# Attention on one core: the last key tile's product with V as two 64-column halves

## The chip, the cores and the metric

The kernel runs on one core of one Trainium2 chip. The metric is the device time in microseconds (us) of one launch; lower is better. Three runs of the kernel before gave a median of 579.14 us (578.97 to 582.09).

## The reference

Four batches, eight heads, 576 positions, head dimension 64, everything in float32. Attention with a position bias is followed by a mixture of experts that takes one expert per token:

```python
scores = scale * np.matmul(q, k.transpose(0, 1, 3, 2))
...
h = np.maximum(x @ w1 + b1, 0.0)
bias = h @ w2
scores = scores + bias.transpose(2, 0, 1)[None, :, :, :]
scores = scores - np.max(scores, axis=-1, keepdims=True)
attn = np.exp(scores)
attn = attn / (np.sum(attn, axis=-1, keepdims=True) + 1e-09)
return np.matmul(attn, v).astype(np.float32)
```

The second half picks an expert `e` for each token from a gate and computes `p[e] * (np.maximum(x @ w1[e], 0) @ w2[e])`. The change concerns only `np.matmul(attn, v)`.

## The kernel before

Heads are taken two at a time: a pair `(p, b)` is two heads `x = 0, 1` of batch `b`. The 576 queries of a pair are five tiles `qt` (four of 128 rows, one of 64 in which both heads share the 128 partitions). For a query tile and head, `emit_s` makes the scores with fp16 matmuls (lines 305 and 306; line 316 for the tile of 64), VectorE adds the bias and takes the row extreme (line 325, one instruction and a short read of its accumulator), and ScalarE takes the exponential (line 330). `emit_t` turns the exponentials over in four transposes on TensorE (line 389) that ScalarE copies out (lines 395 and 393) into `eT`, plus one for key tile 4, the last 64 keys of both heads (lines 403 and 405), which VectorE copies into slot 8 of `eT` (line 406).

`emit_av(p, b, g)` then multiplies with V for a group `g` of query tiles: 256 queries for `g = 0`, 320 for `g = 1`. V is the stationary operand and `eT` the moving one, both float32; a float32 matmul shows as two records in the trace. The result `av` has head 0 in partitions 0 to 63 and head 1 in 64 to 127. Key tiles 0 to 3 belong to one head each, so each is one matmul onto 64 of the 128 columns of TensorE (line 420, `128*64` in the profile), head 0 and head 1 in turn, eight in all. Key tile 4 holds keys of head 0 in its upper 64 rows and keys of head 1 in its lower 64; its V, `vt[:, 4]`, has zeros where head and rows don't match, so one matmul over all 128 columns (line 417, `128*128`) serves both heads and stands first. For `g = 1` a small matmul with 64 columns (line 416) that folds two row sums stands in front of it. VectorE copies `av` out into `xt` (line 429, and line 431 for the folded sums); `av` is a single buffer. `emit_rows` turns `xt` over again (lines 443 and 445).

There are 16 pairs. Eight of them (the list `DMP`) do group 0 in another way, in fp16 with a transposing DMA (lines 346, 350, and 360 to 373 in `emit_lo` and `av_pieces`), so `emit_av` is called 24 times: 8 for `g = 0`, 16 for `g = 1`.

What sets the order: up to the last three units of the attention part the program's text does not. A scheduler takes the instructions of all steps and gives each engine its own order from costs of its own; SyncE's is fixed in the stretch of the `DMP` pairs, and everything from the last three units on stands as it is written. So the matmuls of one `emit_av` call can be parted by matmuls of other steps, and a change of one of them can move instructions on other engines.

## Time and profile before

| | |
|---|---|
| median of three runs | 579.14 us (578.97 to 582.09) |
| the profiled execution: its own time, its span | 580.73 us, 578.9 us |
| PE (TensorE matmul) busy | 533.2 us, 92% of the span |
| DVE (VectorE) busy | 464.8 us, 80% |
| ACT (ScalarE) busy | 436.5 us, 75% |
| POOL (GpSimd) busy | 269.7 us, 47% |
| mean granted TensorE clock | 0.983 of full speed |

The profiled execution's own time is the span and 1.8 us around it. The bias and first scores take the time up to about 60 us, attention goes on to about 340 us, and the experts take the rest. A busy PE is not PE at its peak: matmuls are pipelined, and the end of each is modelled. So the time that a matmul really takes from the engine is read from the starts of neighbours.

### The profile page before, as it was taken

What the parts mean: (1) busy time and instruction counts of PE and PEld (TensorE: products, weight loads), DVE (VectorE), ACT (ScalarE), POOL (GpSimd) and SP (SyncE); (2) the same over time, 40 slices, a digit from 0 to 9 for tenths busy, and PEclk for the clock granted to TensorE, in tenths of its full rate; (3) what the DMA queues carried; (4) which work ended last, traced back from release to release, by engine and by line L of the source; (5) the groups of instructions that cost most, each with busy time, mean ns of one, the idle gap of its engine ahead of it and who ended that gap; (6) DMA issues with size and microseconds to landing.
All of it is one profiled execution on the core that took longest, in us unless ns stands there. A gap on an engine that the chain in (4) does not pass through costs nothing. (4 is left out here: it accounts for less than half of the span.)

```text
span 578.9 us, 14247 instructions
## 1 busy us (share of the span) xinstructions
PE 533.2 (92%) x5302; PEld 358.7 (62%) x5319; DVE 464.8 (80%) x913; ACT 436.5 (75%) x743; POOL 269.7 (47%) x293
## 2 busy tenths in 40 slices
PE   4667999999999999999999999999999999999992
PEld 1223445665666667767577777487776867777851
DVE  7986886688888888787977558869999799897960
ACT  5876887866978877877689965468998787886940
POOL 5200000695199969966744760622344554344111
PEclk9998999999999999999999998799999999999997
DMA  8765447765698799845165002765999968889050
GB/s 284 257 183 166 116 138 209 235 201 145 168 246 226 194 259 241 224 103 151 62 243 154 11 23 59 241 227 194 296 269 267 336 155 214 156 214 236 16 185 30
DMA packets 99613, 106.15 MB, mean 183 GB/s; under 512 B 66893, under 2 KB 76239, under 8 KB 95442
## 3 DMA queue, kind: packets, MB, share of 16 engines
q1 hardware_dynamic: 94752, 89.45, 55.4%
q0 software_dynamic: 4640, 15.43, 8.9%
q8 instruction: 44, 0.72, 0.5%
q14 instruction: 31, 0.25, 0.2%
q10 hardware_dynamic: 146, 0.30, 0.2%
HBM read 128.92 MB, written 20.80 MB: 259 GB/s over the span
## 5 line engine op out<-in xcount | busy, mean ns | idle before, releaser
L330 ACT ACTIVATE e<-e,st 128x576 f32<-128x576 f32 x144 | 111.6, 776 | 14.4 <-DVE st L325 13.2
L325 DVE CUSTOM_DVE_ANT_0 e<-sps,wb 128x576 f32<-128x576 f32 x144 | 106.8, 750 | 16.9 <-PE sps L306 8.1
L1002 POOL DMA_INDIRECT out_dram<-y,odx x17 | 34.2, 2011 | 85.6 <-ACT y L992 45.5
L305 PE MATMUL sps<-kh,qs 128*128 128x288 f16 x256 | 68.5, 289 | 5.5 <-DVE st L325 3.9
L905 DVE TENSOR_TENSOR w<-wb,w 128x2048 bf16<-128x2048 f32 (+1 forms) x36 | 72.2, 2048 | 1.6 <-ACT w L898 1.4
L389 PE MATMUL ta<-c_cpb,e 128*128 128x128 f32 x448 | 71.2, 280 | 0.9 <-ACT e L330 0.4
L395 ACT COPY eT<-ta 128x512 f32<-128x512 f32 x96 | 54.9, 581 | 21.4 <-PE ta L389 20.0
L306 PE MATMUL sps<-kl,qs 128*128 128x288 f16 x256 | 67.8, 287 | 0.0
L976 PE MATMUL yp<-w,hhT 128*128 128x512 f16 (+1 forms) x255 | 64.4, 384 | 1.1 <-issue 0.2
L898 ACT CAST w<-wb 128x2048 f16<-128x2048 f32 (+1 forms) x40 | 63.8, 1639 | 2.2 <-DMA wb<-in_w_dram 1.3
L420 PE MATMUL av<-eT,vt 128*64 128x320 f32 (+1 forms) x384 | 62.4, 424 | 0.0
L937 PEld LDWEIGHTS <-we 128*128 128x128 f16 (+1 forms) x1056 | 59.9, 98 | 3.0 <-issue 0.5
L937 PE MATMUL sps<-xT,we 128*128 128x128 f16 (+1 forms) x1056 | 61.2, 219 | 0.0
L389 PEld LDWEIGHTS ta<-c_cpb,e 128*128 128x128 f32 x448 | 52.3, 142 | 12.8 <-ACT eT L395 3.0
L210 PE MATMUL sps<-hd,c_cpa 128*32 128x512 f32 (+17 forms) x352 | 43.7, 494 | 17.4 <-DVE hd L196 10.7
L196 DVE TENSOR_SCALAR hd<-tab,bp 128x448 f32<-128x448 f32 (+17 forms) x129 | 49.9, 446 | 5.0 <-PE sps L210 4.7
L937 PE MATMUL sps<-xT,wb 128*128 128x128 f16 (+3 forms) x1056 | 50.1, 209 | 0.6 <-issue 0.6
L937 PEld LDWEIGHTS <-wb 128*128 128x128 f16 (+1 forms) x1056 | 48.1, 99 | 3.7 <-issue 2.4
L905 DVE TENSOR_TENSOR we<-ws,we 128x2048 bf16<-128x2048 f32 (+1 forms) x25 | 48.7, 1985 | 0.0
L976 PEld LDWEIGHTS <-hhT 128*128 128x128 f16 x272 | 26.2, 100 | 29.9 <-issue 2.6
L118 POOL TENSOR_TENSOR qs<-qf,qs 64x288 f16<-64x288 f32 x48 | 42.8, 911 | 1.7
L420 PEld LDWEIGHTS av<-eT,vt 128*64 128x64 f32 x384 | 26.9, 136 | 26.5 <-issue 8.7
(234 smaller groups left out, 1013.9 us busy)
## 6 DMA issues: line engine op xcount, KB each, us to landing
ws<-in_w_dram SPq DMA_DIRECT2D x34, 1024.0 KB
wb<-in_w_dram SPq DMA_DIRECT2D x34, 1024.0 KB
hs<-in_w_dram SPq DMA_DIRECT2D x20, 1024.0 KB
bias_d<-bv SPq DMA_DIRECT2D x36, 295.5 KB
kf<-in_kt_dram SPq DMA_DIRECT2D x24, 288.0 KB
wb<-bias_d SPq DMA_DIRECT2D x16, 288.0 KB
wb<-bias_d SPq DMA_DIRECT2D x16, 256.0 KB
xrow_d<-xo SPq DMA_DIRECT2D x16, 256.0 KB
```

What stands on the lines that cost most here:

```text
L196: nc.vector.tensor_scalar(out=hd[:, 0:n], in0=tab[:, 0:n], scalar1=bp[:, k:k + 1], scalar2=0.0, op0=ALU.add, op1=ALU.max,)
L305: nc.tensor.matmul(out=ps[:, half, 0:288], lhsT=lq, rhs=kh[:, j], start=True, stop=False)
L306: nc.tensor.matmul(out=ps[:, half, 0:288], lhsT=lq, rhs=kl[:, j], start=False, stop=True)
L325: nc.vector.tensor_tensor_reduce(out=e, in0=ps[:, :, 0:288], in1=bsl, scale=-0.125, scalar=1e30, op0=ALU.add, op1=ALU.min, accum_out=st[:, ...
L330: nc.scalar.activation(out=e, in_=e, func=AF.Exp, scale=-1.0, bias=st[:, 0:1], accum_out=sm)
L389: nc.tensor.transpose(out=ta[:, j, :], in_=e[:, o:o + 128], identity=ident)
L395: nc.scalar.copy(out=eTv[:, :, hh, o:o + 128], in_=ta)
L420: nc.tensor.matmul(out=av[64 * x:64 * x + 64, 0:n], lhsT=vt[:, j, 64 * x:64 * x + 64], rhs=eT[:, 2 * j + x, 0:n], start=False, stop=(j == 3),)
L898: nc.scalar.copy(out=wh[c][:, sl], in_=src)
L905: nc.vector.tensor_tensor(out=wl[c][:, sl], in0=src, in1=wh[c][:, sl], op=ALU.subtract)
L937: nc.tensor.matmul(out=hp.rearrange("p a j -> p (a j)")[:, n * f:n * f + n], lhsT=w[f // 4][:, o:o + 128], rhs=x[:, kt], start=(i == 0), s ...
L976: nc.tensor.matmul(out=yp, lhsT=x[:, kt], rhs=w[kt // 4][:, 512 * (kt % 4):512 * (kt % 4) + 512], start=(i == 0), stop=(i == len(terms) - 1),)
```

## The change

The full-width matmul of key tile 4 goes. In its place two matmuls of 64 columns each, one per head, stand in front of the others, in one loop with them. They read the same rows of `eT` and the two column halves of the same `vt[:, 4]`.

```diff
         if g == 1:
             av_t[p, b] = av
             nc.tensor.matmul(out=av[0:64, 320:322], lhsT=fold, rhs=hs_t.pop((p, b)), start=True, stop=True)
-        nc.tensor.matmul(out=av[:, 0:n], lhsT=vt[:, 4], rhs=eT[:, 8, 0:n], start=True, stop=False)
-        for j in range(4):
+        for j in (4, 0, 1, 2, 3):
             for x in range(2):
                 nc.tensor.matmul(
                     out=av[64 * x:64 * x + 64, 0:n], lhsT=vt[:, j, 64 * x:64 * x + 64],
-                    rhs=eT[:, 2 * j + x, 0:n], start=False, stop=(j == 3),
+                    rhs=eT[:, 8 if j == 4 else 2 * j + x, 0:n], start=(j == 4), stop=(j == 3),
                 )
```

In the changed file the matmuls of the loop are line 419, and every later line has a number one lower (442 for 443, and so on). In the lists below an engine's instructions stand in its order, with line, operation, output and inputs, and the size of the output; "x8" is eight in a row.

TensorE, one `emit_av` call with `g = 1` at about 138 us. Before:

```order
L443 MATMUL ta<-c_cpb,xt 128x128 x4
L445 MATMUL tb_r<-c_cpb,xt 64x128
L416 MATMUL av<-hs,c_cpb 64x2
L417 MATMUL av<-eT,vt 128x320
L420 MATMUL av<-eT,vt 64x320 x8
L488 MATMUL sps<-xt,c_cpb 32x288 x6
```

And with the change:

```order
L442 MATMUL ta<-c_cpb,xt 128x128 x4
L444 MATMUL tb_r<-c_cpb,xt 64x128
L416 MATMUL av<-hs,c_cpb 64x2
L419 MATMUL av<-eT,vt 64x320 x10
L487 MATMUL sps<-xt,c_cpb 32x288 x6
```

Here all ten halves follow the small matmul of line 416, and no full-width matmul stands between.

TensorE, the first `emit_av` call with `g = 1`, at about 111 us. Before:

```order
L306 MATMUL sps<-kl,qs 128x288
L417 MATMUL av<-eT,vt 128x320
L389 MATMUL ta<-c_cpb,e 128x128 x4
L420 MATMUL av<-eT,vt 64x320 x8
L305 LDWEIGHTS qs
```

And with the change:

```order
L306 MATMUL sps<-kl,qs 128x288
L419 MATMUL av<-eT,vt 64x320
L389 MATMUL ta<-c_cpb,e 128x128 x4
L419 MATMUL av<-eT,vt 64x320 x9
L305 LDWEIGHTS qs
```

The first half took the place of the full-width matmul, four transposes stand behind it, and the second half of key tile 4 is the first of the nine that follow.

VectorE at about 153 us, in the stretch of the `DMP` pairs (`e_1933` and `e_1941` are the same fp16 buffer under two numbers). Before:

```order
L373 COPY xt<-av 128x256
L325 ISA e,st<-sps,wb_127 128x576
L325 ISA st 128x1
L346 TENSOR_TENSOR e_1933<-e,e_1933 128x1152
L406 COPY eT<-tb_r 128x64
```

And with the change:

```order
L373 COPY xt<-av 128x256
L325 ISA e,st<-sps,wb_127 128x576
L325 ISA st 128x1
L406 COPY eT<-tb_r 128x64
L325 ISA e,st<-sps,wb_127 128x576
L325 ISA st 128x1
L346 TENSOR_TENSOR e_1941<-e,e_1941 128x1152
```

The copy into slot 8 of `eT` now stands in front of the subtraction of line 346, and so does the next tile's instruction of line 325.

## Rows read from the trace of the kernel before

**Rows 1.** Busy time by stretch; columns PE, PEld, DVE, ACT, POOL, clock, DMA, GB/s.

```profile
60.00:105.00 45.00, 44.44 (x372) 23.60 (x368) 33.91 (x92) 36.07 (x84) 0.50 (x4) 1.00 0.59 168
105.00:150.00 45.00, 42.16 (x332) 27.62 (x330) 36.37 (x93) 32.16 (x75) 31.63 (x40) 1.00 0.65 187
150.00:265.00 115.00, 110.70 (x947) 76.20 (x944) 96.66 (x255) 95.15 (x220) 89.97 (x98) 1.00 0.80 202
265.00:340.00 75.00, 73.67 (x598) 51.16 (x596) 52.26 (x167) 59.78 (x132) 48.46 (x68) 1.00 0.37 118
```

**Rows 2.** Lines 420 and 417: records, shortest, median and longest ns, first and last start.

```profile
L420 PE MATMUL av<-eT,vt x384: 379/432/484, 63.7 to 338.7; 128*64 128x320 f32 x128, 128*64 128x256 f32 x64
...
L417 PE MATMUL av<-eT,vt x48: 379/432/537, 63.2 to 336.3; 128*128 128x320 f32 x32, 128*128 128x256 f32 x16
```

**Rows 3.** Order of time on PE, 111 to 115 us: start, duration, instruction, records.

```profile
111.31 0.70 PE L417 MATMUL av<-eT,vt 128*128 128x320 f32 x2
111.85 0.60 PE L389 MATMUL ta<-c_cpb,e 128*128 128x128 f32 x4
112.38 2.37 PE L420 MATMUL av<-eT,vt 128*64 128x320 f32 x16
114.69 0.30 PE L305 MATMUL sps<-kh,qs 128*128 128x288 f16 x1
```

**Rows 4.** Order of time on PE, 93 to 96 us, with 256 queries.

```profile
93.35 0.65 PE L420 MATMUL av<-eT,vt 128*64 128x256 f32 x4
93.93 1.28 PE L210 MATMUL sps<-hd,c_cpa 128*32 128x512 f32 x16
95.14 0.65 PE L420 MATMUL av<-eT,vt 128*64 128x256 f32 x2
95.72 0.44 PE L389 MATMUL ta<-c_cpb,e 128*128 128x128 f32 x2
```

**Rows 5.** Order of time on PE, 153 to 157 us.

```profile
153.94 0.28 PE L305 MATMUL sps<-kh,qs 128*128 128x288 f16 x1
154.06 0.28 PE L306 MATMUL sps<-kl,qs 128*128 128x288 f16 x1
155.17 0.81 PE L417 MATMUL av<-eT,vt 128*128 128x320 f32 x2 [0.82 <-DVE eT L406]
155.91 0.75 PE L420 MATMUL av<-eT,vt 128*64 128x320 f32 x2
156.59 0.30 PE L305 MATMUL sps<-kh,qs 128*128 128x288 f16 x1
```

**Rows 6.** Order of time on PE, 138 to 142 us.

```profile
138.31 0.28 PE L416 MATMUL av<-hs,c_cpb 128*64 128x2 f32 x2
138.52 0.81 PE L417 MATMUL av<-eT,vt 128*128 128x320 f32 x2
139.25 2.37 PE L420 MATMUL av<-eT,vt 128*64 128x320 f32 x16
141.56 1.82 PE L488 MATMUL sps<-xt,c_cpb 128*32 128x288 f32 x12
```

**Rows 7.** Order of time on PE, 266 to 267 us.

```profile
266.25 0.81 PE L417 MATMUL av<-eT,vt 128*128 128x320 f32 x2
266.90 0.60 PE L389 MATMUL ta<-c_cpb,e 128*128 128x128 f32 x4
```

**Rows 8.** Order of time on DVE, 153 to 156 us.

```profile
153.56 0.08 DVE L325 DVE_READ_ACCUMULATOR2_ANT st<- 128x1 f32 x1
153.62 1.36 DVE L346 TENSOR_TENSOR e<-e,e 128x1152 f16<-128x1152 f32 x1
154.90 0.22 DVE L406 COPY eT<-tb_r 128x64 f32<-128x64 f32 x1
155.03 0.75 DVE L325 CUSTOM_DVE_ANT_0 e<-sps,wb 128x576 f32<-128x576 f32 x1
```

**Rows 9.** Order of time on PE, 166 to 168 us: the next use of the transposing DMA's result.

```profile
166.87 0.49 PE L360 MATMUL av<-eT,v 128*128 128x256 f16 x3
```

**Rows 10.** Waits on PE, 105 to 340 us: us in total, times, longest.

```profile
PE av L417 <- DVE eT L406: 1.7, 3, 0.8
...
PE av L416 <- DVE xt L373: 0.7, 1, 0.7
```

**Rows 11.** Busy time by stretch, behind the attention part; columns as in rows 1.

```profile
354.00:361.00 7.00, 7.00 (x69) 4.93 (x66) 6.90 (x13) 3.16 (x9) 0.00 (x0) 0.76 0.24 37
```

## The prediction

> **What bounds the kernel now.** I began with busy time by stretch, because the change sits in attention alone. [...] The idle time left in 150 to 265 us is 115 - 110.70 = 4.3 us; no order of work can win more there. Line 417 has 48 records, two to a matmul, hence 24 calls, and line 420 has 384, hence 192 halves [rows 2]. What each costs I then read from starts in order of time, not from durations, which overlap.

> **Prices, from starts.** A full-width matmul of 320 queries between other full-width work holds PE for 111.85 - 111.31 = 0.54 us [rows 3]. Eight halves of the same size hold it for 114.69 - 112.38 = 2.31 us [rows 3]; one half alone holds it for 156.59 - 155.91 = 0.68 us [rows 5]. So the eight go as four pairs, 0.68 + 3 x 0.54 = 2.30: two halves side by side cost 0.54 us, as much as one full-width matmul, and the block has 0.14 us around it. With 256 queries the rows say it directly: two halves hold PE for 93.93 - 93.35 = 0.58 us, one alone for 95.72 - 95.14 = 0.58 us [rows 4]. **A half alone costs what a pair costs.** That is the key of this change: ten halves in one block are five slots, as one full-width and eight halves were; ten halves parted into one and nine are 1 + 5 = six.

> Going from full width to 64 columns costs something too. Line 417 behind line 416 holds PE for 266.90 - 266.25 = 0.65 us if full-width work follows [rows 7], and for 139.25 - 138.52 = 0.73 us if halves follow [rows 6]: 0.08 us more. With the 0.14 us around a block, a pass into 64 columns and back costs 0.22 us.

> [...]

> **The change, part by part.** I went through the 24 places in the two orders.

> (a) Eight places read 416, 417, eight of 420, and now 416 and the halves in one run (in four of them score matmuls part the run, as they did before, and the slots stay as many). Before: 0.21 + 0.73 + 2.31 = 3.25 us from line 416 to the end [rows 6]. Now the halves' five slots take 0.68 + 4 x 0.54 = 2.84, and line 416 something between nothing and its old 0.21 us; its 0.21 us holds a change of width of 0.08, so I take 0.12. That is 2.96, a gain of 0.29 a place; the ends are 0.20 and 0.41. At two of the eight, line 417 waits for DVE's copy of line 406 (two of the three waits in [rows 10]), which hides what is gained in front of it: 0.20 there. Sum: 6 x 0.29 + 2 x 0.20 = **-2.1 us** (-1.6 to -3.3).

> (b) At five places the two halves of key tile 4 are parted (one, other work, then nine, or four and five with three places in between): one slot more each, 5 x 0.54 = **+2.7 us**.

> (c) Five more calls start 416, 417 and then go on with something else; now 416 and one half. 0.21 + 0.65 = 0.86 [rows 6, 7] becomes 0.12 + 0.68 = 0.80: **-0.3 us** over the five.

> (d) Three places had line 417 between full-width work, at no change of width, and now have a half, or both, there: +0.22 each, and at one a score matmul is cut off behind the block, +0.1: **+0.8 us**.

> (e) At one place a run of 16-column matmuls is cut in two by a half, +0.2; at another a score block of line 316 that had been cut by lines 443 and 445 is whole again, -0.2. **0.**

> (f) Seven places keep slots and widths. **0.**

> PE's work: -2.1 + 2.7 - 0.3 + 0.8 = **+1.1 us**.

> **Waits.** The scheduler also moved other instructions. At 153.62 us DVE begins the subtraction of line 346, and the copy of line 406 behind it ends at 154.90 + 0.22 = 155.12 [rows 8]; line 417 waits for it, and so 1.11 us lie between the last score matmul's start at 154.06 and its own at 155.17, where 154.06 - 153.94 = 0.12 is the pitch [rows 5]. With the change line 406 stands in front of line 346, so it can end about 153.84. **-1.0 us** (0 to -1.0). Line 346 moves back by one line 325 and its read, 0.75 + 0.08 us [rows 8]; its result goes through a transposing DMA to line 360, which runs at 166.87 without a wait [rows 9], 13 us behind 153.62, so I cost that at nothing; if that cover is gone it is 0.8 us. The next call waits at line 416 for line 373, 0.7 us [rows 10]; there one score matmul and a small transpose now stand in front and fill part of the wait: **-0.3 us** (0 to -0.7). SP's and POOL's orders are unchanged. DVE's copy of line 429 still follows the last half, and its readers come one block later by (b); where they wait, PE has score matmuls in front of them.

> **Sum.** +1.1 - 1.0 - 0.3 = -0.2 us. The profiled execution took 580.73 us, so 580.5; it stands 1.6 us above the median of 579.14, so against that median I predict **578.9 us**. The bounds: below, -1.2 in (a) and -0.4 at the second wait; above, +0.5 in (a), +1.0 and +0.3 for waits that stay and +0.8 for line 346. All on one side they give 577.3 and 581.5.

> **Rivals.**
> 1. Faster. PE's idle time comes from the scheduler's order, and the new order happens to have less. For it: one move that I found takes 1.0 us; against it: PE has only 4.3 us of idle time in that stretch [rows 1], and only one other move meets a listed wait. If all 4.3 us went: +1.1 - 4.3 = -3.2, so 575.9 us.
> 2. Slower, by waits: the order's other moves lengthen waits instead. Line 346 goes back at one place, and the copy of line 406 goes behind lines 346 and 373 at the next. If the two waits stay and two new ones of 0.8 us (line 346's delay) come: +1.1 + 1.6 = +2.7, 581.8 us. [...] Against it: the two places are all that I found for it.
> 3. Slower, by one mechanism: the two halves of key tile 4 read the same rows of `eT` at the same time, and every pair of the rows above reads two different tiles. If they can't go side by side, each of the 19 calls in which they stand together pays a slot more, about 0.5 us: +9.5 us, 588.4 us. It decides from 0.15 us a call on (19 x 0.15 = 2.9). Against it: nothing shows such a bar; for it: no row shows such a pair.

> That the change does not do what it says is true in part, and in the sum: in five of 24 calls the halves are not side by side (b).

> **How the numbers follow.** 0.5% is 2.9 us here, about what a measurement of this kernel can tell from no change: below 576.2 is faster, above 582.0 slower. My forecast has 0.72, rival 1 0.10, rival 2 0.12 (half of it above 582.0), rival 3 0.06. Faster: rival 1 and a little of the forecast's lower side, 0.11. Slower: rival 3, half of rival 2 and 0.05 of the forecast's upper side (one of the three runs before was 582.09), 0.17. Same: 0.72. The range reaches into both waiting rivals and leaves rival 3 out: 576.0 to 582.5.

> **What would show it.** In the changed profile: no line 417, and 480 records at line 419; blocks of ten halves of 320 queries from start to next start 2.84 us (with rival 3 about 3.4); a gap of 0.08 to 0.21 us between line 416 and the first half; no wait of 1 us near 154 us; PE's busy time in 60 to 340 us about 1 us higher for the same work; the waits at lines 360 and 416 no longer than now. The prediction is wrong if the experts' part changes by more than 2 us, or if the attention part's end moves by more than 2 us with blocks at these prices.

## The result, and the profile after

The changed kernel takes 587.03 us (median of 22 runs, 583.69 to 591.48), the kernel before on the same chip 580.88 us (22 runs, 577.07 to 587.11). The ratio is 1.0102, 95% interval [1.008, 1.0125]: about 6 us slower. (A ratio here leaves out executions over 1.5% above the fastest of the same kernel, so it can differ from the quotient of two medians.) The prediction was 578.9 us with a range up to 582.5. The profiled execution took 586.98 us with a span of 585.2 us, against 580.73 and 578.9 before.

First the busy time of the four stretches of attention, columns as in [rows 1].

```profile
60.00:105.00 45.00, 44.44 (x374) 23.12 (x372) 34.16 (x94) 35.95 (x83) 0.49 (x4) 1.00 0.60 166
105.00:150.00 45.00, 43.46 (x352) 29.04 (x348) 35.74 (x93) 33.02 (x76) 31.51 (x40) 1.00 0.69 189
150.00:265.00 115.00, 107.69 (x926) 75.45 (x921) 95.61 (x244) 91.88 (x211) 89.56 (x98) 0.99 0.78 201
265.00:340.00 75.00, 73.30 (x602) 50.81 (x601) 53.72 (x173) 59.51 (x132) 44.92 (x64) 1.00 0.39 120
```

PE has not become busier from 150 to 265 us; it lost 110.70 - 107.69 = 3.0 us of busy time there, and the clock of the stretch is no longer 1.00. The time went into waiting, not into work. Over the four stretches PE is busy for 268.89 of 280 us, where it had been 270.97 [rows 1].

The prices of the work itself are as forecast. PE in order of time, a block of ten halves at 137 us (to hold against [rows 6]), then at 110 us a call whose two halves lie parted ([rows 3]):

```profile
137.28 0.22 PE L416 MATMUL av<-hs,c_cpb 128*64 128x2 f32 x1
137.29 0.48 PE L419 MATMUL av<-eT,vt 128*64 128x320 f32 x1
137.36 0.20 PE L416 MATMUL av<-hs,c_cpb 128*64 128x2 f32 x1
137.41 2.88 PE L419 MATMUL av<-eT,vt 128*64 128x320 f32 x19
140.23 1.16 PE L487 MATMUL sps<-xt,c_cpb 128*32 128x288 f32 x6
```

```profile
110.87 0.75 PE L419 MATMUL av<-eT,vt 128*64 128x320 f32 x2
111.55 0.66 PE L389 MATMUL ta<-c_cpb,e 128*128 128x128 f32 x4
112.13 2.91 PE L419 MATMUL av<-eT,vt 128*64 128x320 f32 x18
114.97 0.30 PE L305 MATMUL sps<-kh,qs 128*128 128x288 f16 x1
```

From line 416 to the end of the ten: 140.23 - 137.28 = 2.95 us (forecast 2.96). The two records of line 416 and the first of line 419 alternate, so the small matmul and the first half overlap; where a gap of 0.08 to 0.21 us was expected between them, 0.13 us lie from line 416 to the nineteen records that follow. A half alone: 0.68 us; nine in a block: 114.97 - 112.13 = 2.84 us, five slots.

What is new is a wait. PE's waits from 105 to 340 us, in us, times and longest, the rows that answer to [rows 10]:

```profile
PE av L360 <- DMA eT<-e: 4.8, 4, 2.1
PE sps L305 <- DVE st L325: 1.8, 3, 1.2
PE sps L756 <- DVE cs L682: 1.4, 1, 1.4
PE av L419 <- DVE eT L406: 1.3, 2, 0.7
```

Line 360 waited 0.9 us, once, before (at 215.87 us). Its longest wait now is where [rows 9] had none:

```profile
169.00 0.80 PE L360 MATMUL av<-eT,v 128*128 128x256 f16 x3 [2.05 <-DMA eT<-e]
```

And with this wait TensorE's clock falls. Two stretches of 4 us, of the changed kernel and then of the kernel before; columns as in [rows 1]:

```profile
164.00:168.00 4.00, 2.56 (x19) 1.84 (x18) 2.85 (x10) 4.00 (x11) 3.91 (x6) 1.00 1.22 187
168.00:172.00 4.00, 3.00 (x25) 2.17 (x26) 1.58 (x1) 2.33 (x5) 4.00 (x4) 0.58 0.93 332
```

```profile
164.00:168.00 4.00, 4.00 (x43) 2.99 (x43) 3.01 (x12) 4.00 (x10) 4.00 (x6) 1.00 1.07 271
168.00:172.00 4.00, 3.28 (x29) 1.73 (x24) 3.26 (x6) 3.65 (x9) 3.92 (x4) 1.00 0.75 189
```

The granted clock is 0.58 over 168 to 172 us; in the trace's clock records it is 0.50 for 3.41 us from 168.62 us on, 0.38 us before the wait ends, and 1.00 on both sides. As an estimate from these, that is worth up to 0.42 x 4 = 1.7 us. The DMA share over 164 to 168 us, 1.22 and 1.07, is above 1 in both kernels (so the times of packets overlap) and shows no slack, but the changed one moved 187 GB/s where the other had moved 271.

Why they moved less is in the DMA view of 163 to 168 us: 40 slices of 0.125 us, the busy share in tenths, the GB/s, and the queues. The changed kernel:

```profile
DMA  3899889999999999999999989000100000499999
GB/s 111 258 350 313 276 307 340 379 363 430 360 356 232 271 269 285 266 324 182 262 264 272 205 20 12 0 0 4 8 8 10 8 10 10 96 293 287 287 285 293
...
q8 instruction: 1, 0.02, 1.7%
```

The kernel before:

```profile
DMA  7999999969999999999999975368896999899897
GB/s 279 340 314 256 260 268 209 131 113 219 289 293 283 295 289 289 293 291 293 283 293 312 137 86 37 55 166 240 332 258 240 387 387 442 350 387 406 313 350 258
...
q1 hardware_dynamic: 2840, 1.34, 110.3%
```

In the changed kernel next to nothing moves for some 1.3 us, from 166.0 to 167.25. There is one transfer on q8 of the kind "instruction" in the window; in the kernel before there is none, and q1 is its only queue. By the trace's DMA records it is one packet of 16 KB, from 165.12 to 166.46: the stop begins 0.9 us behind its start and lasts until 0.8 us behind its end. In the kernel before the packet that corresponds to it begins at 169.47. Over the whole execution q8 brings 44 of them:

```profile
PE 537.0 (92%) x5350; PEld 362.3 (62%) x5367; DVE 467.1 (80%) x913; ACT 436.9 (75%) x743; POOL 259.9 (44%) x293
...
q8 instruction: 44, 0.72, 0.5%
```

5350 + 5367 records of PE to 44 packets are 244 a packet; by the trace, with TensorE's semaphore and few other records counted too, 255.6 start from one packet to the next, the mean of the first 41 such stretches (254.1 in the kernel before). So my theory, A in the expectations below, became: **q8 brings TensorE's program, one block per 256 instructions or so, and one block now falls into a transposing DMA that line 360 needs.** The change adds 48 matmul records, and as many weight loads, over the attention part, and so each block is fetched at an earlier place of the work.

The rivals, B: VectorE's new order (line 346 later, the prediction's own doubt) makes the transposing DMA late; the new order is worse in some other way; or the halves cost more than their slots.

### The profile page after: what moved, and what is told of

It reads as the page before. It is cut to its first block, busy times and chain, and to the rows that moved or that the text cites. A ratio compares the mean times of both kernels' runs of the same rounds, so it can differ in the third digit from the quotient of the medians.

```text
span 585.2 us, 14341 instructions
## 1 busy us (share of the span) xinstructions
PE 537.0 (92%) x5350; PEld 362.3 (62%) x5367; DVE 467.1 (80%) x913; ACT 436.9 (75%) x743; POOL 259.9 (44%) x293
## 5 line engine op out<-in xcount | busy, mean ns | idle before, releaser
L419 PE MATMUL av<-eT,vt 128*64 128x320 f32 (+1 forms) x480 | 79.8, 423 | 1.3 <-DVE eT L406 1.3
L1001 POOL DMA_INDIRECT out_dram<-y,odx x17 | 31.3, 1841 | 85.9 <-ACT y L991 62.7
L210 PE MATMUL sps<-hd,c_cpa 128*32 128x512 f32 (+17 forms) x352 | 45.1, 507 | 16.9 <-DVE hd L196 10.7
L419 PEld LDWEIGHTS av<-eT,vt 128*64 128x64 f32 x480 | 38.1, 136 | 24.4 <-issue 7.1
L897 ACT CAST we<-ws 128x2048 f16<-128x2048 f32 (+1 forms) x26 | 41.4, 1637 | 0.0
```

Of the source, the lines that this page charges most:

```text
L419: nc.tensor.matmul(out=av[64 * x:64 * x + 64, 0:n], lhsT=vt[:, j, 64 * x:64 * x + 64], rhs=eT[:, 8 if j == 4 else 2 * j + x, 0:n], start=( ...
L897: nc.scalar.copy(out=wh[c][:, sl], in_=src)
```

## The experiments

Each kernel ran beside the kernel before, on the same chip; "us" is a median, and the ratios of one group share the runs of before. All force the order of the instructions of each engine by a table, through this piece, which adds order and no wait:

```diff
+    ...
+    link = mybir.DependencyInfo(mybir.DependencyClass.NoSync, mybir.DependencyReason.DATA)
+    for name, table in ORDER.items():
+        traced = [i for i in nc.cur_bb.bb.instructions if i.engine == kinds[name]]
+        place = [traced[k] for at, n in table for k in range(at, at + n)]
+        ...
+        for one, two in zip(place, place[1:]):
+            tc.add_manual_dep(two, one.name, link, reason="order")
     fin = ExitStack()
```

### Order and halves apart

At this point the code block was not in my theories; I weighed order against halves. **halves_old_order** has the changed matmuls in the order of the kernel before:

```diff
 ORDER["PE"], the first call with g = 1, at about 111 us:
-L419 (half), L389 x4, L419 x9
+L419 x2,     L389 x4, L419 x8
```

> The changed matmuls, but every engine held to the order that the kernel before has; the two halves of key tile 4 stand together where the full-width matmul stood, so no slot is added. Theory order (the halves cost what the starts said; the loss is waits that the new order makes): 1.7 us faster than before (0.5 to 3), from -2.1 where line 416 stands in front, -0.3 where it stands in front and other work follows, +0.7 at the three places between full-width work. Theory halves (the two halves with the same moving rows, or something in the matmuls themselves, is slow): 4 to 6 us slower than before, as the changed kernel.

Measured: 582.9 us, ratio 0.9994 [0.9961, 1.0026]. The loss is gone by the ratio (the median is 0.3% above that of the kernel before, 581.0 us), so the halves as such are not what costs 6 us; but the forecast gain of 1.7 us, 0.5 at least, does not show either.

**full_new_order** has the full-width matmul back, in the place of the first half (at 111 us as below), and everything else in the changed kernel's order:

```diff
-L419,        L389 x4, L419 x9
+L417 (full), L389 x4, L420 x8
```

> The matmuls of before, with the full-width matmul where the first half stood, and every engine held to the order of the changed kernel. Theory order: 3 to 6 us slower than before, since the wait for the transposing DMA at line 360 near 167 us comes without any half; PE's own work is as before within 0.5 us. Theory halves: as before, within 1 us.

Measured: 581.29 us, ratio 0.9983 [0.9949, 1.0018]. The order theory missed: with the order complete, line 346 behind line 406 among it, nothing is lost.

So neither half of the change shows a cost alone. **new_order_old_at_150** and **old_order_new_at_150** cut the order by place: changed matmuls, and the stretch from 148 to 176 us in one order, the rest in the other.

```diff
 ORDER of PE, DVE, ACT, POOL with the changed matmuls:
-new order everywhere
+new order, but old order from 148 to 176 us     (new_order_old_at_150)
+old order, but new order from 148 to 176 us     (old_order_new_at_150)
```

> The changed kernel held to its own order, except that from about 148 to 176 us all engines have the order of before. Theory order, with the loss at line 360: about 2.5 us slower than before (1 to 4), that is 3.5 us faster than the changed kernel. If the order matters but the place is another: 6 us slower, as the changed kernel. Theory halves: 6 us slower too.

> The changed matmuls held to the order of before, except that from about 148 to 176 us all engines have the new order. Theory order, with the loss at line 360: 3.5 us slower than the halves in the old order, so about 2 us slower than before (0.5 to 3.5), with a wait of some 2 us at line 360 near 167 us. If the place is another: as the halves in the old order. Theory halves: 4 to 6 us slower than before.

Measured: 585.48 us, 1.0035 [0.999, 1.0079], and 586.19 us, 1.0054 [1.0012, 1.0096]. As ratios both, 2.0 and 3.1 us, are what the order theory had. The first is the least certain here: its median is 1.0077 times that of the kernel before. What speaks against that theory is the trace. With the old order restored where the loss is, line 360 still waits:

```profile
169.23 0.49 PE L360 MATMUL av<-eT,v 128*128 128x256 f16 x3 [2.56 <-DMA eT<-e]
```

In this kernel the first transposing DMA of the pair was issued at 155.53, earlier than before, and the second at 162.71, as late as in the changed kernel (162.87; before 161.58). Moving line 346 back did not make the second transfer earlier: SyncE's queue was held by the first one for 5.51 us (4.15 before), and the second follows 1.7 us behind that hold in each of these kernels. That took the blame from line 346, and sent me to the DMA records and the code blocks.

### Moving the code blocks

The next eight kernels change no work. They put tiny matmuls on an unused tile ahead of everything, where PE would be idle (its first matmul starts at 5.41 us in the kernel before and at 5.49 in the changed one), so that every later block is fetched at another place of the work:

```diff
     tb_r = tb_ps.tile([128, 512], F32, name="tb_r")
+    pad16 = const.tile([128, 32], F16, name="pad16")
+    nc.gpsimd.memset(pad16, 0.0)
+    for _ in range(96):
+        nc.tensor.matmul(out=tb_r[0:32, 0:2], lhsT=pad16, rhs=pad16[:, 0:2], start=True, stop=True)
```

The count is 96 here, and 32, 80, 112 or 128 in others. Each is two instructions, one weight load and one matmul; the four added lines make line 360 line 364 there.

> The changed kernel with 96 tiny matmuls (192 TensorE instructions with their weight loads) on an unused tile ahead of everything else; all else in the changed kernel's own order. Theory A (code block): TensorE's program is brought in blocks of 16 KB, about one per 256 instructions. In the changed kernel's trace one such block is fetched at 165.12 us, in the middle of the second transposing DMA (its 256-byte packets run from 164.3 to 168.4 and all but stop from 166.0 to 167.2), line 360 then waits 2.05 us and the clock falls to 0.58 over 168 to 172; in the kernel before the block comes at 169.47, after the transposing DMA. 192 instructions more put the block 64 instructions later, to about 169 us: 580 to 583 us, ratio to the kernel before 0.998 to 1.004, line 360 waits under 1 us near 167. Theory B (order: line 346 later on VectorE, or the column halves themselves): the padding changes nothing, 586 to 588 us, ratio 1.008 to 1.013.

> The changed kernel in its own order with 128 tiny matmuls (256 instructions, one whole code block) ahead of everything else: the control for the padding of 192. Theory A (a code block fetched inside the transposing DMA near 167 us): every later block lies where it lay, so one is fetched again inside the second transposing DMA's packets, they take 4.0 us rather than 2.9, line 360 waits 1.5 to 3 us and the whole is 586 to 589 us, ratio 1.008 to 1.014. Theory P (the padding changes something at the start and that is what helped): as with 192, 581 to 584 us.

> The changed kernel in its own order with 160 more instructions at the start. Theory A: the block goes 96 instructions, some 6 us, later than in the changed kernel, to about 171 us, well behind the transposing DMA, and the block of 118 us to about 124, behind the load of V that was late by 2.7 us in the kernel with 192 more: 579 to 582.5 us, ratio 0.998 to 1.003. Theory P: no difference to 192 beyond 0.5 us. Theory B (order or halves cost by themselves): 586 to 588 us.

Measured: 192 more 582.67 us, 1.0035 [1.0003, 1.0068]; 256 more 584.97 us, 1.0075 [1.0044, 1.0105]; 160 more 584.36 us, 1.004 [1.0007, 1.0074]. With 256, one whole block, the ratio is a little below the 1.008 to 1.014 expected; the packet is back at 165.10 us (165.12 in the changed kernel), and so are the wait and the lower clock; with 192 it lies at 167.67, behind the transfer, and both are gone. PE at line 360 and the clock behind it, with 256:

```profile
169.44 0.49 PE L364 MATMUL av<-eT,v 128*128 128x256 f16 x3 [2.72 <-DMA eT<-e]
```

```profile
168.00:172.00 4.00, 2.56 (x29) 1.85 (x28) 1.76 (x2) 2.15 (x5) 4.00 (x3) 0.85 1.03 344
172.00:176.00 4.00, 4.00 (x23) 2.13 (x22) 2.92 (x7) 2.08 (x5) 3.78 (x6) 0.72 0.92 226
```

And with 192:

```profile
164.53 0.49 PE L364 MATMUL av<-eT,v 128*128 128x256 f16 x3
```

```profile
168.00:172.00 4.00, 4.00 (x28) 2.14 (x29) 3.19 (x11) 2.82 (x6) 3.79 (x5) 1.00 1.00 204
172.00:176.00 4.00, 4.00 (x34) 2.78 (x32) 3.75 (x11) 2.58 (x9) 3.91 (x5) 1.00 0.99 240
```

That q8 follows TensorE's instruction count, and that the place of its blocks decides this wait, is shown by these two. With 160 line 360 near 167 us doesn't wait either, but the whole came out above my expectation. The DMA records of that execution show blocks inside three other transposing DMAs, which begin at 138.75, 172.54 and 204.12 us: their 2304 packets take 3.5 to 3.6 us each (2.3 is the median of those without a block, over all kernels).

The same on the kernel before, and on the halves in its order:

> The kernel before, in its own order, with 32 tiny matmuls (64 instructions) ahead of everything else. Theory A: the code block that came at 169.47 us comes 64 instructions earlier, at about 165 us, into the transposing DMA: line 360 near 167 us waits 1 to 2.5 us, 584 to 587 us, ratio 1.005 to 1.011, without any change to the halves or the order. Theory B: as the kernel before, 580 to 582 us, ratio 0.998 to 1.002.

> The kernel before with 128 tiny matmuls (256 instructions, a whole block) ahead of everything else. Theory A: every later block is fetched where it was, near 169.5 us: 580.5 to 583 us, where up to 2 us would be the padding's own price at the start. If padding as such is what costs, it is slower than the kernel with 64 more instructions.

> The kernel before in its own order with 160 more instructions at the start, for the comparison with the column halves at the same padding. Theory A: its blocks go 96 instructions later, or 160 earlier, than without padding: from 169.5 to about 159 us, into the loads and the first transposing DMA: 582 to 586 us. If alignment of code blocks matters at one place of the changed kernel alone: 580.5 to 582 us.

> The column halves in the order of the kernel before (both halves where the full-width matmul was), with 192 more instructions ahead of everything else. Without the padding it took 582.9 us, its block came at 167.04 us, at the end of the transposing DMA. Theory A: the block goes to about 171 us, and the saved switches show: 578 to 581 us, ratio 0.995 to 1.0. Theory B: as without the padding, 582 to 583.5 us.

> The column halves in the order of the kernel before, with 160 more instructions at the start. Theory A: with 192 more it lost 5 us near 121 us, where a load of V landed behind a code block; with 160 that block goes to about 125 us and the other to about 173 us: 577 to 580.5 us, ratio 0.992 to 0.999, the first version faster than the kernel before. If the saved switches are given back whatever the code blocks do: 581 to 583 us.

Measured, all three within what was expected of the time, the kernel before with 64, 160 and 256 more: 584.27 us, 1.0064 [1.0035, 1.0094]; 582.22 us, 1.0045 [1.0017, 1.0072]; 582.48 us, 1.0032 [0.9997, 1.0068]. The kernel before can be made 0.64% slower by 64 instructions that compute nothing. With 64 the block does fall into the transposing DMA (at 166.57), whose packets take 4.2 us instead of 2.8, but line 360 waits only 0.58 us there, short of the 1 to 2.5 expected. Over the whole attention part it waits five times, 4.9 us in all, against once, 0.9 us, in the kernel before; the longest are 1.71 us at 152.88 and 1.47 at 219.75. The halves in the old order: 580.94 us, 0.999 [0.9955, 1.0026] with 192, and 580.1 us, 0.9996 [0.9963, 1.0029] with 160. The 580.94 is as expected; with 160 the ratio should have been 0.992 to 0.999, and that gain did not come. At equal padding of 160 the halves stand at 0.9996 and the full-width kernel at 1.0045; one pair of runs is too little to call that the halves' gain.

The kernel before with 160 more shows a second way for a block to reach line 360 (line 364 there). One is fetched from 203.29 to 204.85 us, among plain loads, and SyncE's queue is held 1.78 us by a load that takes 0.43 in the kernel before; the transposing DMA behind it is issued at 208.16 (208.04 before), although PE is 1.3 us ahead:

```profile
203.43 1.78 SPq L171 DMA_DIRECT2D wb<-bias_d  x1
```

```profile
216.00 0.82 PE L364 MATMUL av<-eT,v 128*128 128x256 f16 x3 [2.30 <-DMA eT<-e]
```

In the kernel before that wait is the 0.92 us at 215.87. Behind the 2.30 us the granted clock is 0.63 over 216 to 220 us, and the execution loses 2.4 us between 215 and 225. No run moved this block alone.

With 192 in the old order another place lost time. VectorE near 121 us:

```profile
121.61 0.97 DVE L280 CAST v<-vt 128x640 f16<-128x640 f32 x1 [5.32 <-DMA vt<-in_vl_dram]
```

A load of V was late by 5 us, with a block fetched at 118.07. Whether the block delayed it, I have not shown.

### The parted halves

What was left over with 192 more (1.0035) could be the halves that lie parted, or the order. Both halves go to the first one's place in the new order; only PE's order changes:

```diff
 ORDER["PE"], new order, at three of the eight places where the halves lay parted:
-L419,    L389 x4, L419 x9
+L419 x2, L389 x4, L419 x8
```

> The changed kernel in its own order, but with the second column half directly behind the first at the eight places where they lay parted; no padding. If parted halves cost what the prediction took (0.54 us at each of five places): 2.7 us less than the changed kernel, 583.5 to 585 us, ratio 1.004 to 1.008, with line 360 still waiting 1.5 us or more near 167 us, since the block of code lies where it did. If parted halves cost nothing: 586 to 588 us. If they are all of it: 580 to 581.5 us with no wait at line 360.

> The same with 192 more instructions at the start, so that the block lies behind the transposing DMA. The changed kernel with that padding took 582.7 us, ratio 1.0035. Theory A with the price of parted halves: 2.7 us less, 579 to 581 us, ratio 0.997 to 1.001. If the new order itself, not the parting, is what was left: 582 to 583.5 us.

> The column halves in the order of the kernel before, with 224 more instructions, so that the block near 167 us lies 32 later than without padding, 169 us and more, where the kernel before has it. Theory A: 578 to 580.5 us, ratio 0.994 to 1.0. If the saved switches are given back at transfers whatever the blocks do: 580 to 583 us.

Measured: 583.68 us, 1.0059 [1.0024, 1.0094] without padding, where line 360 still waits; 580.0 us, 0.9999 [0.996, 1.0037] with 192. Both came out where the price of parted halves puts them. The price itself stands in the rows: behind the two halves and the four transposes the block that took 114.97 - 112.13 = 2.84 us in the changed kernel takes 117.80 - 115.50 = 2.30, one slot less.

```profile
114.22 0.76 PE L419 MATMUL av<-eT,vt 128*64 128x320 f32 x4
114.91 0.66 PE L389 MATMUL ta<-c_cpb,e 128*128 128x128 f32 x4
115.50 2.38 PE L419 MATMUL av<-eT,vt 128*64 128x320 f32 x16
117.80 0.30 PE L305 MATMUL sps<-kh,qs 128*128 128x288 f16 x1
```

The halves in the old order with 224: 579.58 us, 0.9978 [0.9943, 1.0012], the lowest of all, and still within what can be told from no change. No version beats the kernel before for certain.

PE near 171 us without padding: the wait is there, but a little shorter, and the clock stays.

```profile
171.31 0.49 PE L360 MATMUL av<-eT,v 128*128 128x256 f16 x3 [1.89 <-DMA eT<-e]
```

```profile
172.00:176.00 4.00, 4.00 (x44) 2.57 (x39) 3.13 (x8) 2.00 (x5) 3.92 (x4) 1.00 0.95 287
```

### All of them in one table

The second transposing DMA before line 360: time from its first to its last 256-byte packet (2432 of them each time), the block of q8 that is nearest, line 360's wait, and the ratio. Sorted by the first column.

```
kernel                   packets, from .. to       us   block at   wait   ratio
after_pad160             164.37 .. 166.93         2.56   173.16    0.00   1.0040
before_pad160            162.06 .. 164.65         2.59   156.85    0.10   1.0045
old_order_pad160         161.85 .. 164.62         2.77   168.69    0.41   0.9996
before                   163.16 .. 165.95         2.79   169.47    0.00   1
new_order_old_at_150     164.31 .. 167.14         2.83   166.88    2.56   1.0035
pairs_pad192             164.06 .. 166.89         2.83   169.78    0.08   0.9999
full_new_order           163.62 .. 166.48         2.86   170.03    0.00   0.9983
old_order_pad192         168.87 .. 171.75         2.88   175.65    0.73   0.9990
before_pad256            168.28 .. 171.18         2.90   173.89    0.04   1.0032
old_order_pad224         166.98 .. 169.95         2.97   172.10    0.28   0.9978
halves_old_order         164.32 .. 167.30         2.98   167.04    0.27   0.9994
after_pad192             160.94 .. 164.01         3.07   167.67    0.09   1.0035
pairs_new_order          166.79 .. 170.75         3.96   167.52    1.89   1.0059
after                    164.44 .. 168.42         3.98   165.12    2.05   1.0102
before_pad64             166.12 .. 170.29         4.17   166.57    0.58   1.0064
old_order_new_at_150     166.54 .. 170.81         4.27   167.28    2.46   1.0054
after_pad256             163.95 .. 168.68         4.73   165.10    2.72   1.0075
```

Where a block begins well inside, the packets take 4.0 to 4.7 us; elsewhere 2.6 to 3.1. The same holds beyond this transfer. In the 17 traces a block begins 0.1 to 1.3 us into a transposing DMA of 2304 packets ten times, and the packets take 3.5 to 4.1 us; 161 such transfers without a block have a median of 2.3 us, and three of them reach 3.5. Each time the packets go on for 0.4 to 1.2 us behind the block's start and then all but stop. A block is not the only thing that slows them: those of 2432 packets that begin between 223 and 231 us take 4.2 to 4.9 us without one.

The five kernels of the first kind have the five highest ratios, 1.0054 to 1.0102, though the next, 1.0045, is within the intervals. All five wait 4.0 to 6.5 us at line 360 in the attention part as a whole; so does new_order_old_at_150 (4.7), and the eleven others wait 0 to 3.2 us. In new_order_old_at_150 the block begins as the last packets go; they end in time, but line 360 starts 2.1 us after the last of them, where the others that wait need 0.5 to 0.8. A transfer ends with 32 records of 4 bytes, and the last two of these come at 167.97 there, 0.8 us behind the last packet; in halves_old_order, where the block begins as late (167.04), all 32 are there by 167.32 and line 360 starts 0.5 us behind the last packet. That these records hold back line 360 is my reading, not shown.

Last, where each execution gained and lost: the start of the same instruction of line 330 on ACT, against the kernel before, in us.

```
before     after   pairs_new_order   after_pad192   pairs_pad192   old_order_pad224
 72.60     +0.12        +3.13           -2.00          -1.93            -0.02
149.24     -1.28        +2.24           -1.77          +0.48            +2.52
158.87     +0.75        +3.32           -1.96          +0.76            +3.22
168.74     -0.32        +2.14           -2.83          +0.06            +3.21
179.17     +2.84        +3.74           -2.70          +0.20            +3.11
263.17     +3.17        +3.99           -1.96          +0.25            +3.12
297.30     +5.01        +5.22           +0.04          +0.29            +2.85
323.77     +5.02        +5.22           +0.05          +0.29            +2.81
```

The first line is what the start of the kernel, before attention, does from one execution to another (-2.0 to +3.1); read each column downwards from there. Between 168.74 and 179.17 the changed kernel loses 3.2 us, pairs_new_order, whose clock stays, 1.6, and the other three nothing. Of the five parted places with a slot more two lie near 111 and 117 us and three behind 263 us: between 263 and 271 us the changed kernel loses 0.79 and from 285 to 297 us 0.66, pairs_new_order 0.23 and nothing. (It loses 1.0 in between, 271 to 285; PE's waits at lines 756 and 671, for VectorE, are 1.4 and 0.7 us there, 0.7 and 0.3 in the kernel before.) pairs_pad192 gives back early what it wins there: it loses 2.4 us between 99 and 122 us, where VectorE's cast of V waits 4.05 us for its load, 1.18 in the kernel before.

## Why the prediction was wrong, point by point

**Step (a), blocks of ten, and the key that a half alone costs a pair: right.** 2.95 us against 2.96 a block; 0.68 and 2.84 us for parted halves. Up to 149 us the changed kernel is 1.4 us ahead (+0.12 to -1.28); not all of that is (a), since full_new_order, without halves, is 0.8 ahead there (+1.61 to +0.85).

**Step (b), five parted places, +2.7 us: right in the price, and the sum agrees.** A slot of 0.54 us goes where the halves are put together (2.84 to 2.30). The ratio goes from 1.0102 to 1.0059 without padding and from 1.0035 to 0.9999 with it, 2.5 and 2.1 us; the intervals are some 0.35% each way, so the second difference alone can't be told from zero, and the first holds more than the slots: between 169 and 179 us, where the clock fell in one kernel and not in the other, the profiled executions differ by 1.6 us. Steps (c) and (d) were not tried alone.

**The wait at line 417 near 154 us, -1.0 us: the wait went, the gain did not come.** PE's lead of 1.28 us ran into a transfer. Line 468 on ACT, the cast into `xo`, stands in front of the cast of line 336 in the new order, no longer behind it, and has to wait for the store of the tile before it to leave; VectorE's line 124 waits for line 468, and PE's line 305 for VectorE:

```profile
151.73 0.72 ACT L468 CAST xo<-xr 128x640 f16<-128x640 f32 x1 [2.43 <-DMA xrow_d<-xo]
```

```profile
152.48 0.83 DVE L124 TENSOR_TENSOR xo<-xr,xo 128x640 bf16<-128x640 f32 x1 [3.77 <-ACT xo L468]
```

```profile
154.37 0.28 PE L305 MATMUL sps<-kh,qs 128*128 128x288 f16 x1 [1.21 <-DVE st L325]
```

That store left SyncE's queue at 146.70 us, 0.45 later than before, behind a transposing DMA that held the queue for 4.22 us (3.71 before). PE's gain did not bring that store forward. The same chain goes on: the store behind line 124 leaves at 153.34 (152.66 before), and the loads and the first transposing DMA of the pair behind it 0.7 us later than before, at 156.46.

**The step that failed: the transposing DMA costed at nothing.** The prediction put line 360 "13 us behind" the subtraction of line 346 and took that for cover. Line 360 needs both transposing DMAs of its pair, and the second belongs to the next subtraction, at 158.65, so even that distance was 8 us. The cover that counts is from the transfer's landing to line 360. The records of the kernel before have the last packet at 165.95; with the 0.5 to 0.8 us that kernels which wait show from the last packet to line 360's start, line 360 could have run from 166.45 to 166.75 on, and it ran at 166.87: **0.1 to 0.4 us of cover, not 13.** My bound "if that cover is gone it is 0.8 us" named the right instruction, but for a wrong reason. Line 346's move is not it: with the move undone line 360 waited 2.56 us in new_order_old_at_150, and full_new_order has it without a loss. What takes the time from 153 us on is, as I read it, the 16 DMA engines, whose share is 0.91 to 1.22 in both kernels over 155 to 160, 160 to 164 and 164 to 168 us; no run took load off them.

In the changed kernel PE came to line 360 at 166.95. Of its wait of 2.05 us about 1.0 is the code block (packets over 3.98 us instead of some 2.95), and the other 1.0 a transfer that was issued 1.3 us later than before, less the cover: 0.7 us of it come down the chain from line 468, and 0.6 from the first transposing DMA, which held the queue 4.74 us (4.15 before). For the place of the code blocks the prediction had no term at all. Behind it the clock costs up to 1.7 us, by the estimate above: pairs_new_order, with a wait of 1.89 us and no loss of clock, loses 1.6 us there and the changed kernel 3.2. In ratios, moving the block away is worth 1.0102 - 1.0035 = 0.67%, 3.9 us, or 1.0075 - 1.0035 = 0.40%, 2.3 us, against the padding of 256, and in the kernel with the halves together 0.60%, 3.5 us; each difference has an interval of some 0.4% each way. The padding moves every block, not this one alone: line 360's waits in all go from 4.8 to 0.3 us.

**Rival 2, slower by waits, came nearest.** Two waits went and two others came, 1.21 and 2.05 us where it took 0.8 each, plus a stretch of 3.41 us at a granted clock of 0.50 (up to 1.7 us, by the same estimate). Its reason (line 346 and line 406 in another order) was not the one. **Rival 3 is refuted:** halves that read the same rows of `eT` do go side by side; ten take five slots (2.95 us with line 416 in front of them). **Rival 1** had idle time leaving PE; in 150 to 265 us it grew from 4.3 to 7.3 us.

**What would show it wrong** was met as written: the end of the attention part moved by 5 us (+5.02 at 323.77) with blocks at their forecast prices.

So of the 6 us, by the ratios: some 2.3 to 3.9 go with where the blocks of code lie, most of it (3.2 us of the profiled execution) at the transposing DMA near 165 us with the wait and the clock behind it, 2 to 2.5 the parted halves, and the rest of the new order comes to nothing that can be measured (1.3 of the 6.3 us come behind attention in the profiled execution; the experts' part was not taken apart). The forecast saving of the old-order version, 1.7 us, can't be told from zero in four alignments (0.9978 to 0.9996). What stays open: how much of the kernel before's loss with each of the three paddings comes from its blocks (with 64 and 160 more it waits longer at line 360, with 256 it loses 1.8 us near 121 us), and what delayed the load of V there.

## What to carry to other kernels

Where DMA engines are as full as here (a share of 0.91 to 1.22), cover is measured from the landing of the transfer to its reader, out of the DMA records; the distance between the instructions on both sides of it, 8 or 13 us here, did not show that 0.1 to 0.4 us were left. A change that adds instructions to a long unrolled program can also move where its blocks of code are fetched, here from 169.47 to 165.12 us, so a difference of 0.5% may be neither the work nor the order (64 instructions that compute nothing made the kernel before 0.64% slower); a control that adds instructions which compute nothing (some part of a block, and a whole block) tells it. And a wait on PE can cost more than its length when the clock goes down behind it: 3.2 us in the changed kernel for a wait of 2.05 with the clock at 0.50 behind it, against 1.6 in pairs_new_order for one of 1.89 with the clock at 1.00.

## What I had not expected of the hardware

The clock fell to 0.58 and 0.72 to 0.85 (means of 4 us) behind waits of 2.05 and 2.72 us, and to 0.63 behind one of 2.30 us in the kernel before with 160 more; it stayed at 1.00 behind one of 1.89 us.
